# A grouped-query decode kernel: the values of the last three pairs multiplied in narrow pieces, and the last load cut in six

## The chip, the cores and the metric

The kernel runs on one core of one Trainium2 chip. The metric is the device time of one execution in microseconds (us), as a median over runs. Everything is float32.

## The reference

A decode step: eight sequences, one new token each. Attention with 32 query heads over 8 key/value heads and 8192 cached positions, plus a token-mixing block and the input itself. Cut to what matters:

```
x  = A_x                                        # 8 x 1 x 512
xn = layernorm(x)
q  = xn @ wq                                    # 32 heads of 128
s  = q . k_cache * 128**-0.5                    # per sequence and head, 8192 positions
p  = softmax(s)
o  = p . v_cache                                # per sequence and head, 128 wide
out = x + concat(o) @ wo + mixer(xn)            # mixer: layernorm, x*w1 + b1, gelu, times w2, sum, + b2
```

The key and the value cache hold 8 x 8 x 8192 x 128 numbers each, 512 MB together. They are read once.

## The kernel before

**Pairs and chunks.** The work is 64 pairs `i` of one key/value head and one sequence (`N_IT`). A pair has a key tile and a value tile of 4 MB each, [128 partitions x 64 tokens x 128], loaded by one DMA each into a ring of five buffers (`RING`, tile name `raw`). A pair is worked on in four chunks (`NCH`) of 16 tokens per partition (`CH_T`), so the whole has 256 chunks `n`. The DMAs are issued from SP, in an order sorted ahead; each waits until its ring buffer has been read for the last time. The very last load, the values of pair 63, goes out in five DMAs: 32 tokens of each partition, then 16, 8, 4 and 4.

**One step of the loop.** Step `s` transposes the keys of chunk `s+1` on TensorE (`t_half`, L202, copied out of PSUM by ACT and DVE at L203), multiplies the keys of chunk `s` with the query (`qk`, L220), and multiplies the values of chunk `s-9` with the softmax weights (`pv`, `LAG` = 9). Hooks hung on the steps do the softmax of a pair (`sm_max`, `sm_bias` L233, `sm_exp` L242, `sm_place` L249/L250, `sm_sum` L257), put a finished pair into its place (`o_place`, L301, L303), and project a finished head (`o_project`, L309). The order of instructions on each engine is that of this code. After step 255 no keys are left, and the steps hold only `pv` and hooks.

**The values product.** A float32 matmul stands as two records in the trace, and so does its weight load. In `pv` a chunk is four matmuls (`j`), each with 32 columns of weights (a slice of `PT`: four key tokens `u` times four heads, and 16 columns that nobody reads) and 512 wide moving values (four tokens of 128). They go to four column groups of the array, 32 columns each, which the rows show as the form 128*32, and run side by side. Of a result only the blocks count in which the weight's token and the value's token are the same. They stand in four places of a 512 wide PSUM tile: ACT copies and scales it at L289, and `o_place` picks the blocks with four matmuls against the selector `ohu` and adds them up. The last chunk alone (n = 255) is cut further: each of its four matmuls is done as four of 128 wide moving values (L281), which go to column group `u`, with the same weights and still a 512 wide result. Its copy out of PSUM is done in two halves of 256.

**The end.** Pair 63 is followed by `o_place(63)`, the projection of the last head (L309), an addition on DVE (L311) and the store of the output (L391).

Of the kernel before, what the change touches and what calls it, by code (L numbers as in the profile page):

```python
# [8 lines left out]
F32 = mybir.dt.float32  # L9
AF = mybir.ActivationFunctionType  # L10
# [4 lines left out]
B, D, HQ, HKV, SK, DH, F = 8, 512, 32, 8, 8192, 128, 1792  # L15
REP = HQ // HKV
P = 128
NT = SK // P
CH_T = 16
NCH = NT // CH_T  # L20
CG = 4
GT = CH_T // CG
GW = P // CG
# [5 lines left out]
N_IT = B * HKV  # L29
NK = N_IT * NCH  # L30
ZO = (NCH - 1) * 2 * REP
ZW = ZO + GW
PW = CG * NCH * GT * REP
LAG = 9
RING = 5

# [2 lines left out]
def attn_mixer_kernel(ctx: ExitStack, tc: tile.TileContext, x, kc, vc, wq, wo, w1, b1, w2, b2, out):  # L39
    nc = tc.nc  # L40
    const = ctx.enter_context(tc.tile_pool(name="const", bufs=1))
# [10 lines left out]
    def misc():  # L52
        return ps_m.tile([P, 512], F32, name="misc")
# [4 lines left out]
    for i in range(N_IT):  # L58
        order.append((i * NCH - 1, kc, KR, i))
        order.append((i * NCH + LAG, vc, VR, i))  # L60
    order.sort(key=lambda o: -o[0])

    def load_next():
        if order:
            _, src, to, i = order.pop()
            h, b = divmod(i, B)
            t = ring.tile([P, NT, DH], F32, name="raw")
            rows = src[b, h].rearrange("(p t) d -> p t d", p=P)
            first, last = to is KR and not i, not order
            at = 0  # L70
            for n in (CH_T,) * NCH if first else (NT // 2, CH_T, 2 * GT, GT, GT) if last else (NT,):
                nc.sync.dma_start(t[:, at:at + n, :], rows[:, at:at + n, :])
                if first and not at:
                    load_wq(0)
                at += n
            to[i] = t
# [3 lines left out]
    def load_wq(h):  # L80
        w = REP * DH
        t = one.tile([P, NC, w], F32, name="wqo")
        nc.sync.dma_start(t, wq[:, h * w:(h + 1) * w].rearrange("(c p) n -> p c n", p=P))
        wqs[h] = t

    def load_wo(h):
        t = one.tile([P, REP, D], F32, name="wqo")
        nc.sync.dma_start(t, wo[h * REP * DH:(h + 1) * REP * DH, :].rearrange("(r p) n -> p r n", p=P))
        wos[h] = t

    load_next()
    x_sb = t2k.tile([B, D], F32, name="t2k")
    nc.scalar.dma_start(x_sb, x.rearrange("b s d -> (b s) d"))
# [6 lines left out]
    for _ in range(RING - 1):  # L100
        load_next()
# [7 lines left out]
    ident = const.tile([P, P], F32, name="ident")  # L109
    make_identity(nc, ident)  # L110

    oh = const.tile([P, REP], F32, name="oh")
    nc.vector.tensor_reduce(oh, ident.rearrange("p (g h) -> p h g", h=REP), AX.X, ALU.add)
    ohw = t2k.tile([P, P], F32, name="t2k")
# [25 lines left out]
        Z.append(z)  # L140
    PT = []
    for k in range(2):
        t = const.tile([P, PW + GW - GT * REP], F32, name=f"pt{k}")
        nc.vector.memset(t, 0.0)
        PT.append(t)
    OTS = []
    for k in range(2):
        t = const.tile([P, REP, GW], F32, name=f"ot{k}")
# [45 lines left out]
    def t_half(n, k):  # L194
        if n >= NK:
            return
        if k == 0:
            KT[n] = ktp.tile([P, CH_T * P], F32, name="kt")
        w = CH_T // 2
        pt = ps_t.tile([P, w * P], F32, name="pt")  # L200
        for t in range(w):
            nc.tensor.transpose(pt[:, t * P:(t + 1) * P], KR[n // NCH][:, n % NCH * CH_T + k * w + t, :], ident)  # L202
        (nc.vector.tensor_copy if k else nc.scalar.copy)(KT[n][:, k * w * P:(k + 1) * w * P], pt)  # L203
        if k and n % NCH == NCH - 1:
            del KR[n // NCH]
            load_next()
# [38 lines left out]
    def sm_place(i):  # L245
        p = st[i][0]
        m = misc()
        for u in range(GT):
            nc.tensor.transpose(m[:, u * P:(u + 1) * P], p[:, u * P:(u + 1) * P], ident)  # L249
        nc.scalar.copy(PT[i % 2][:, :PW].rearrange("p (x u h) -> p x u h", u=GT, h=REP),  # L250
                       m.rearrange("p (u x k h) -> p x k u h", u=GT, k=2, h=REP)[:, :, 0])

    RL = {}
# [9 lines left out]
    O, OB = {}, {}  # L263

    def pv(n):
        if not 0 <= n < NK:
            return
        i, c = divmod(n, NCH)
        if c == 0:
            O[i] = ps_a.tile([P, 512], F32, name="acc")  # L270
        v = VR[i][:, c * CH_T:(c + 1) * CH_T, :].rearrange("p t d -> p (t d)")
        for j in range(CG):
            o = (j * NCH + c) * GT * REP
            w = PT[i % 2][:, o:o + GW]
            if n < NK - 1:
                nc.tensor.matmul(O[i][j * GW:(j + 1) * GW, :], w, v[:, j * 512:(j + 1) * 512],  # L276
                                 start=(c == 0), stop=(c == NCH - 1))
            else:
                for u in range(GT):
                    x = slice(u * DH, (u + 1) * DH)  # L280
                    nc.tensor.matmul(O[i][u * GW:(u + 1) * GW, x], w, v[:, j * 512 + u * DH:j * 512 + (u + 1) * DH],  # L281
                                     start=False, stop=(j == CG - 1))
        if c == NCH - 1:
            del VR[i]
            load_next()
            ob = t2k.tile([P, 512], F32, name="t2k")
            o, rl = O.pop(i), RL.pop(i)
            for x in ((slice(0, 512),) if n < NK - 1 else (slice(0, 256), slice(256, 512))):
                nc.scalar.activation(ob[:, x], o[:, x], AF.Copy, scale=rl)  # L289
            OB[i] = ob  # L290

    OT = {}
# [1 line left out]
    def o_place(i):  # L294
        h, b = divmod(i, B)
        if b == 0:
            OT[h] = OTS[h % 2]
        m = misc()
        ob = OB.pop(i)
        for u in range(GT):  # L300
            nc.tensor.matmul(m[:, :REP], ob[:, u * DH:(u + 1) * DH], ohu[:, u * REP:(u + 1) * REP],  # L301
                             start=(u == 0), stop=(u == GT - 1))
        nc.vector.tensor_copy(OT[h][:, :, BS * b], m[:, :REP])  # L303

    def o_project(h):
# [36 lines left out]
    def at(s, k, f, *a):  # L342
        hooks.setdefault((s, k), []).append((f, a))

    for i in range(N_IT):
        s = (i + 1) * NCH
        at(s - 1, 2, sm_max, i)
        at(s, 3, sm_bias, i)
        at(s + 1, 1, sm_exp, i)
        at(s + 1, 3, sm_place, i)  # L350
        at(s + 2, 3, sm_sum, i)
        at(s + LAG + (2 if i < N_IT - 2 else 0), 3, o_place, i)
    HS = B * NCH
    for h in range(HKV):
        s = h * HS
        if h + 1 < HKV:
            at(s + LAG + 4, 3, load_wq, h + 1)
            at(s + LAG + 9, 2, q_project, h + 1)
            at(s + LAG + 10, 2, q_place, h + 1)
        at(s + LAG + 12, 3, load_wo, h)  # L360
        at(s + HS + LAG + 3, 2, o_project, h)
# [18 lines left out]
    for s in range(NK + LAG + 4):  # L380
        for k in range(4):
            if k < 2:
                t_half(s + 1, k)
            elif k == 2:
                qk(s)
            else:
                pv(s - LAG)
            for f, a in hooks.pop((s, k), []):
                f(*a)
# [29 lines left out]
```

## Time and profile before

| | |
|---|---|
| median of 3 runs | 1308.89 us (1308.6 to 1309.88) |
| the profiled execution, its own time | 1308.48 us |
| its span, first to last instruction | 1306.7 us |
| mean granted TensorE clock | 0.957 |
| busy share PE / PE weight loads / DVE / ACT / POOL | 89% / 55% / 31% / 45% / 17% |
| read from HBM | 553.69 MB, 424 GB/s over the span |

PE is TensorE's matmul side, PEld its weight loads, DVE is VectorE, ACT ScalarE, POOL GpSimd, SP the engine that issues the large DMAs. The span is what the trace shows; the profiled execution's time is 1.8 us longer than it.

### The profile page before, as it was taken

What the parts mean: (1) busy time and instruction counts of PE and PEld (TensorE: products, weight loads), DVE (VectorE), ACT (ScalarE), POOL (GpSimd) and SP (SyncE); (2) the same over time, 40 slices, a digit from 0 to 9 for tenths busy, and PEclk for the clock granted to TensorE, in tenths of its full rate; (3) what the DMA queues carried; (4) which work ended last, traced back from release to release, by engine and by line L of the source; (5) the groups of instructions that cost most, each with busy time, mean ns of one, the idle gap of its engine ahead of it and who ended that gap; (6) DMA issues with size and microseconds to landing.
All of it is one profiled execution on the core that took longest, in us unless ns stands there. A gap on an engine that the chain in (4) does not pass through costs nothing.

```text
span 1306.7 us, 22347 instructions
## 1 busy us (share of the span) xinstructions
PE 1162.4 (89%) x9852; PEld 715.8 (55%) x9852; DVE 407.4 (31%) x646; ACT 587.8 (45%) x740; POOL 227.0 (17%) x242
## 2 busy tenths in 40 slices
PE   6979899798998989979898898998989979899988
PEld 4545555455554655546555555554645546555554
DVE  4423233232332333323333233322323323233321
ACT  2654244552545525445254452554525535255532
POOL 1322002220122201222012220122201221012310
PEclk8999999998999999999999898999989989899999
DMA  9999999999999999999999999999999999999995
GB/s 402 432 431 431 428 430 432 429 429 433 432 431 428 429 431 432 432 433 427 433 432 430 430 429 433 433 431 429 429 431 430 433 429 432 432 432 432 432 427 223
DMA packets 28164, 555.13 MB, mean 425 GB/s; under 512 B 2556, under 2 KB 2588, under 8 KB 11172
## 3 DMA queue, kind: packets, MB, share of 16 engines
q1 hardware_dynamic: 27924, 553.67, 98.8%
q8 instruction: 77, 1.26, 0.4%
q14 instruction: 19, 0.16, 0.0%
q0 software_dynamic: 128, 0.02, 0.0%
q10 hardware_dynamic: 16, 0.02, 0.0%
HBM read 553.69 MB, written 0.02 MB: 424 GB/s over the span
## 4 chain that ended last, share of the span: by engine, by line
DMA 56%; PE 39%; ACT 3%; DVE 1%; issue 1%; POOL 0%; SPq 0%; ACTq 0%; DVEq 0%; POOLq 0%
DMA raw<-in_A_k_cache_dram 37%; DMA wqo<-in_A_wq_dram 17%; PE pt L202 16%; PE acc L220 8%; PE acc L276 8%; PE misc L301 3%; DMA raw<-in_A_v_cache_dram 3%; PE misc L177 1%; ACT L242 1%; PE misc L249 1%; ACT kt L203 1%; ACT t2k L242 1%; PE misc L318 1%; PE misc L257 1%; PE misc L309 1%
## 5 line engine op out<-in xcount | busy, mean ns | idle before, releaser
L202 PE MATMUL pt<-ident,raw 128*128 128x128 f32 x4096 | 515.9, 281 | 67.6 <-DMA raw<-in_A_k_cache_dram 67.1
L202 PEld LDWEIGHTS pt<-ident,raw 128*128 128x128 f32 x4096 | 478.0, 147 | 74.5 <-issue 56.0
L203 DVE COPY kt<-pt 128x1024 f32<-128x1024 f32 x256 | 313.5, 1225 | 618.3 <-PE pt L202 505.4
L203 ACT COPY kt<-pt 128x1024 f32<-128x1024 f32 x256 | 258.8, 1011 | 455.7 <-PE pt L202 322.9
L220 PE MATMUL acc<-kt,z 128*32 128x512 f32 x2048 | 279.0, 617 | 0.0
L276 PE MATMUL acc<-raw,pt 128*32 128x512 f32 x2040 | 273.0, 608 | 2.5 <-DMA raw<-in_A_v_cache_dram 2.5
L329 POOL TENSOR_SCALAR g<-g,w2t 128x512 f32<-128x512 f32 x112 | 77.5, 692 | 876.6 <-ACT g L328 876.6
L276 PEld LDWEIGHTS acc<-raw,pt 128*32 128x32 f32 x2040 | 65.3, 113 | 143.6 <-issue 118.1
L330 POOL TENSOR_TENSOR macc<-macc,g 128x512 f32<-128x512 f32 x112 | 142.3, 1271 | 9.3
L328 ACT ACTIVATE g<-hb,b1t,w1t 128x512 f32<-128x512 f32 x112 | 91.1, 813 | 11.5 <-POOL macc L330 10.9
L289 ACT ACTIVATE t2k<-acc,rl 128x512 f32<-128x512 f32 (+1 forms) x65 | 44.0, 679 | 108.5 <-PE acc L276 104.6
L301 PEld LDWEIGHTS misc<-ohu,t2k 128*128 128x128 f32 x512 | 61.9, 191 | 55.0 <-DVE kt L203 31.0
L249 PEld LDWEIGHTS misc<-ident,t2k 128*128 128x128 f32 x256 | 26.8, 140 | 82.5 <-ACT t2k L242 76.7
L301 PE MATMUL misc<-ohu,t2k 128*128 128x4 f32 x512 | 67.3, 255 | 0.7 <-ACT t2k L289 0.6
L220 PEld LDWEIGHTS acc<-kt,z 128*32 128x32 f32 x2048 | 40.7, 109 | 44.5 <-issue 44.4
L249 PE MATMUL misc<-ident,t2k 128*128 128x128 f32 x256 | 42.0, 286 | 25.5 <-ACT t2k L242 25.5
L242 ACT ACT_TABLE_LOAD x48 | 61.6, 1283 | 0.8
L328 ACT ACT_TABLE_LOAD x48 | 61.6, 1283 | 0.8
L257 PEld LDWEIGHTS misc<-lr,ohl 128*128 128x128 f32 x128 | 20.1, 197 | 59.1 <-issue 50.7
L177 PE MATMUL misc<-wqo,xnT 128*32 128x128 f32 x256 | 15.5, 420 | 38.8 <-DMA wqo<-in_A_wq_dram 38.3
L250 ACT COPY pt<-misc 128x256 f32<-128x256 f32 x64 | 23.7, 370 | 58.1 <-PE misc L249 58.1
L233 PEld LDWEIGHTS misc<-ident,mr 128*128 128x128 f32 x128 | 19.0, 187 | 53.7 <-DVE kt L203 38.6
(67 smaller groups left out, 285.6 us busy)
## 6 DMA issues: line engine op xcount, KB each, us to landing
raw<-in_A_k_cache_dram SPq DMA_DIRECT2D x63, 4096.0 KB, 30.0
raw<-in_A_v_cache_dram SPq DMA_DIRECT2D x63, 4096.0 KB, 33.2
wqo<-in_A_wq_dram SPq DMA_DIRECT2D x8, 1024.0 KB, 30.6
wqo<-in_A_wo_dram SPq DMA_DIRECT2D x8, 1024.0 KB, 28.3
raw<-in_A_k_cache_dram SPq DMA_DIRECT2D x4, 1024.0 KB, 10.2
raw<-in_A_v_cache_dram SPq DMA_DIRECT2D x1, 2048.0 KB, 29.1
raw<-in_A_v_cache_dram SPq DMA_DIRECT2D x1, 1024.0 KB, 31.2
raw<-in_A_v_cache_dram SPq DMA_DIRECT2D x1, 512.0 KB, 31.9
```

The source lines that it names most:

```text
L202: nc.tensor.transpose(pt[:, t * P:(t + 1) * P], KR[n // NCH][:, n % NCH * CH_T + k * w + t, :], ident)
L203: (nc.vector.tensor_copy if k else nc.scalar.copy)(KT[n][:, k * w * P:(k + 1) * w * P], pt)
L220: nc.tensor.matmul(S[i][j * GW:(j + 1) * GW, :], w, kt[:, j * 512:(j + 1) * 512], start=(c == 0), stop=(c == NCH - 1))
L242: nc.scalar.activation(p, S.pop(i), AF.Exp, bias=st[i], scale=SCALE, accum_out=lr)
L249: nc.tensor.transpose(m[:, u * P:(u + 1) * P], p[:, u * P:(u + 1) * P], ident)
L257: nc.tensor.matmul(m[:, :1], ohl, st.pop(i)[1], start=True, stop=True)
L276: nc.tensor.matmul(O[i][j * GW:(j + 1) * GW, :], w, v[:, j * 512:(j + 1) * 512], start=(c == 0), stop=(c == NCH - 1))
L289: nc.scalar.activation(ob[:, x], o[:, x], AF.Copy, scale=rl)
L301: nc.tensor.matmul(m[:, :REP], ob[:, u * DH:(u + 1) * DH], ohu[:, u * REP:(u + 1) * REP], start=(u == 0), stop=(u == GT - 1))
L328: nc.scalar.activation(g, hb, AF.Gelu_apprx_tanh, bias=b1t[:, j:j + 1], scale=w1t[:, j:j + 1])
L329: nc.gpsimd.tensor_scalar(g, g, w2t[:, j:j + 1], 1.0, op0=ALU.mult, op1=ALU.mult)
L330: nc.gpsimd.tensor_add(acc, acc, g)
```

## The change

For the last three pairs (61, 62 and 63; `FINE` = 61) every chunk is done with 16 matmuls of 128 wide values in place of four of 512 (three chunks of pair 63, and all of 61 and 62, had four; the last chunk had 16). The weights slice now begins at the token's own four columns, so the wanted four rows of the result stand at the start of column group `u`, and all tokens of all chunks of a pair accumulate into the same [128 x 128] of PSUM. ACT copies 128 columns instead of 512 (for the last pair: one copy of 128 in place of two of 256), and `o_place` needs one matmul instead of four. `PT` is 12 columns wider, so that the last slice stays inside it; what lies behind it in SBUF moves (in the built program the ring's first buffer starts at byte 29,568 of a partition, 29,440 before). The last load's first DMA of 32 tokens becomes two of 16.

```diff
+FINE = N_IT - 3
...
-            for n in (CH_T,) * NCH if first else (NT // 2, CH_T, 2 * GT, GT, GT) if last else (NT,):
+            for n in (CH_T,) * NCH if first else (CH_T, CH_T, CH_T, 2 * GT, GT, GT) if last else (NT,):
...
-        t = const.tile([P, PW + GW - GT * REP], F32, name=f"pt{k}")
+        t = const.tile([P, PW + GW - REP], F32, name=f"pt{k}")
...
-            w = PT[i % 2][:, o:o + GW]
-            if n < NK - 1:
-                nc.tensor.matmul(O[i][j * GW:(j + 1) * GW, :], w, v[:, j * 512:(j + 1) * 512],
+            if i < FINE:
+                nc.tensor.matmul(O[i][j * GW:(j + 1) * GW, :], PT[i % 2][:, o:o + GW], v[:, j * 512:(j + 1) * 512],
                                  start=(c == 0), stop=(c == NCH - 1))
-            else:
-                for u in range(GT):
-                    x = slice(u * DH, (u + 1) * DH)
-                    nc.tensor.matmul(O[i][u * GW:(u + 1) * GW, x], w, v[:, j * 512 + u * DH:j * 512 + (u + 1) * DH],
-                                     start=False, stop=(j == CG - 1))
+                continue
+            for u in range(GT):
+                w = PT[i % 2][:, o + u * REP:o + u * REP + GW]
+                x = slice((j * GT + u) * DH, (j * GT + u + 1) * DH)
+                nc.tensor.matmul(O[i][u * GW:(u + 1) * GW, :DH], w, v[:, x],
+                                 start=(c == 0 and j == 0), stop=(c == NCH - 1 and j == CG - 1))
...
+            w = 512 if i < FINE else DH
             ob = t2k.tile([P, 512], F32, name="t2k")
-            o, rl = O.pop(i), RL.pop(i)
-            for x in ((slice(0, 512),) if n < NK - 1 else (slice(0, 256), slice(256, 512))):
-                nc.scalar.activation(ob[:, x], o[:, x], AF.Copy, scale=rl)
+            nc.scalar.activation(ob[:, :w], O.pop(i)[:, :w], AF.Copy, scale=RL.pop(i))
...
-        for u in range(GT):
+        n = GT if i < FINE else 1
+        for u in range(n):
             nc.tensor.matmul(m[:, :REP], ob[:, u * DH:(u + 1) * DH], ohu[:, u * REP:(u + 1) * REP],
-                             start=(u == 0), stop=(u == GT - 1))
+                             start=(u == 0), stop=(u == n - 1))
```

PE's order at its end, before, from `sm_sum(63)` on (`acc<-raw,pt` is `pv`, `misc<-ohu,t2k` is `o_place`, `misc<-wqo,ot` the last projection; pairs 61 and 63 use `pt_151`, pair 62 uses `pt_149`, and the shapes are those of the result):

```order
L257 MATMUL misc<-lr,ohl 128x1
L276 MATMUL acc<-raw,pt_149 32x512 x4
L301 MATMUL misc<-ohu,t2k 128x4 x4
L276 MATMUL acc<-raw,pt_149 32x512 x4
L276 MATMUL acc<-raw,pt_151 32x512 x4
L301 MATMUL misc<-ohu,t2k 128x4 x4
L276 MATMUL acc<-raw,pt_151 32x512 x8
L281 MATMUL acc<-raw,pt_151 32x128 x16
L301 MATMUL misc<-ohu,t2k 128x4 x4
L309 MATMUL misc<-wqo,ot_155 32x128 x16
```

and now, at the same place:

```order
L259 MATMUL misc<-lr,ohl 128x1
L283 MATMUL acc<-raw,pt_149 32x128 x16
L303 MATMUL misc<-ohu,t2k 128x4
L283 MATMUL acc<-raw,pt_149 32x128 x16
L283 MATMUL acc<-raw,pt_151 32x128 x16
L303 MATMUL misc<-ohu,t2k 128x4
L283 MATMUL acc<-raw,pt_151 32x128 x48
L303 MATMUL misc<-ohu,t2k 128x4
L311 MATMUL misc<-wqo,ot_155 32x128 x16
```

Nothing has changed its place; each `pv` is 16 narrow matmuls and each of the three `o_place` is one matmul. Lines 32 and later have moved by one or two.

ACT's last rows before (the three copies of pairs 61, 62 and 63 are `t2k<-acc,rl`; `t2k,lr<-acc,nb` is `sm_exp(63)`):

```order
L289 ACTIVATE t2k<-acc,rl 128x512
L242 ACTIVATE t2k,lr<-acc,nb 128x512
L250 COPY pt_151<-misc 128x256
L289 ACTIVATE t2k<-acc,rl 128x512
L289 ACTIVATE t2k<-acc,rl 128x256 x2
```

and now:

```order
L290 ACTIVATE t2k<-acc,rl 128x128
L244 ACTIVATE t2k,lr<-acc,nb 128x512
L252 COPY pt_151<-misc 128x256
L290 ACTIVATE t2k<-acc,rl 128x128 x2
```

The copies are narrower, and the last two have become one. On SP the one row `raw<-in_A_v_cache_dram 128x4096` ahead of the last `128x2048` has become two of `128x2048`; DVE and POOL have the rows that they had.

## Rows read from the trace of the kernel before

**Rows 1.** The page: GB/s in 40 equal slices; a DMA queue: packets, MB, share.

```profile
GB/s 402 432 431 431 428 430 432 429 429 433 432 431 428 429 431 432 432 433 427 433 432 430 430 429 433 433 431 429 429 431 430 433 429 432 432 432 432 432 427 223
...
q8 instruction: 77, 1.26, 0.4%
```

**Rows 2.** Stretches: busy time by engine, granted clock, DMA share, GB/s.

```profile
1270.00:1284.00 14.00, 13.50 (x126) 8.31 (x122) 5.22 (x9) 4.77 (x7) 0.00 (x0) 1.00 0.99 424
1284.00:1298.50 14.50, 14.28 (x118) 6.09 (x114) 2.11 (x9) 2.50 (x5) 0.00 (x0) 1.00 0.51 212
```

**Rows 3.** The chain that ended last, its end: start us, us, what.

```profile
1242.59 36.84 DMA raw<-in_A_v_cache_dram
1279.43 0.14 issue
...
1292.24 0.31 PE misc L257 x2
...
1293.55 0.99 PE misc L301 x8
...
1296.40 1.06 PE misc L301 x8
...
1299.31 0.92 PE acc L281 x32
```

**Rows 4.** SP: DMA of pair 62's values, first and last of pair 63's.

```profile
1257.94 0.33 SPq L72 DMA_DIRECT2D raw<-in_A_v_cache_dram  x1
...
1264.85 0.33 SPq L72 DMA_DIRECT2D raw<-in_A_v_cache_dram  x1
...
1267.36 0.43 SPq L72 DMA_DIRECT2D raw<-in_A_v_cache_dram  x1
```

**Rows 5.** The same three DMAs: KB each, us to landing.

```profile
raw<-in_A_v_cache_dram SPq DMA_DIRECT2D x1, 4096.0 KB, 31.2
...
raw<-in_A_v_cache_dram SPq DMA_DIRECT2D x1, 2048.0 KB, 29.1
...
raw<-in_A_v_cache_dram SPq DMA_DIRECT2D x1, 256.0 KB, 31.7
```

**Rows 6.** L281: ns minimum, median, maximum; first and last start.

```profile
L281 PE MATMUL acc<-raw,pt x32: 272/272/273, 1299.1 to 1299.9; 128*32 128x128 f32 x32
```

**Rows 7.** Timeline: PE in the last pairs, and what follows it.

```profile
1289.31 1.06 PE L276 MATMUL acc<-raw,pt 128*32 128x512 f32 x8
...
1294.46 1.92 PE L276 MATMUL acc<-raw,pt 128*32 128x512 f32 x16
...
1297.38 1.92 PE L276 MATMUL acc<-raw,pt 128*32 128x512 f32 x16
1299.12 1.06 PE L281 MATMUL acc<-raw,pt 128*32 128x128 f32 x32
...
1300.25 0.84 ACT L289 ACTIVATE t2k<-acc,rl 128x256 f32<-128x256 f32 x2 [3.90 <-PE acc L281]
...
1300.77 1.05 PE L301 MATMUL misc<-ohu,t2k 128*128 128x4 f32 x8 [0.59 <-ACT t2k L289]
1301.87 0.17 DVE L303 COPY ot<-misc 128x4 f32<-128x4 f32 x1 [4.21 <-PE misc L301]
```

**Rows 8.** A copy of 128 columns out of PSUM on ACT (L180).

```profile
L180 ACT COPY sq<-misc x8: 265/265/265, 17.6 to 1070.3; 128x128 f32<-128x128 f32 x8
```

**Rows 9.** Timeline: one matmul (L257) and DVE, which waits for it.

```profile
1292.17 0.38 PE L257 MATMUL misc<-lr,ohl 128*128 128x1 f32 x2
...
1292.59 0.17 DVE L259 RECIPROCAL rl<-misc 128x1 f32<-128x1 f32 x1 [2.87 <-PE misc L257]
```

**Rows 10.** L177, 32 matmul records of the narrow form; that stretch.

```profile
1068.34 1.93 PE L177 MATMUL misc<-wqo,xnT 128*32 128x128 f32 x32 [5.51 <-DMA wqo<-in_A_wq_dram]
...
1068.30:1070.30 2.00, 1.96 (x36) 1.93 (x40) 0.00 (x0) 0.00 (x0) 0.00 (x0) 0.50 1.18 508
```

## The prediction

> **What bounds the kernel now.** I read the page first, for what is full all the time. The bytes moved per slice stand at 427 to 433 GB/s from the second slice to the last but one, and fall to 223 in the last [rows 1]: the caches stream at a constant rate, and engines that work less in the middle win nothing. The change does nothing there. It lies in the last 27 us, so the question is what sets the end. The stretches answer the first half: up to 1284 us the DMA engines are busy 0.99 of the time, from 1284 to 1298.5 only 0.51 at 212 GB/s, while PE is busy 14.28 of 14.5 us at a granted clock of 1.00, the 2.4 GHz level [rows 2]. The stream is ragged: about half of the DMA engines are through, and the other half carry the last tile in.
>
> The chain of waits gives the second half. It follows a value DMA to 1279.43, goes 0.14 us later to PE, and stays with PE (short steps of ACT between) to the end of the last chunk at 1299.31 + 0.92 = 1300.23 [rows 3]. By that alone PE sets the end, and each microsecond taken from it would count in full. So I looked at the transfers that the chain doesn't name. Pair 62's values were issued at 1257.94, the first and the last piece of pair 63's at 1264.85 and 1267.36 [rows 4]; 31.2, 29.1 and 31.7 us later they had landed [rows 5], at 1289.14, 1293.95 and about 1299.0. The last chunk's matmuls began at 1299.12 [rows 6, 7]. So PE and the last 256 KB arrive there together, and a faster PE finds a wall 0.1 us ahead of it. That is what the reader is to see: the chain names one bound, and a second stands right behind it.
>
> **The change, part by part.**
>
> *The narrow matmuls.* Eleven chunks go from 8 records of 512 to 32 of 128; the last chunk has the form already, so it has a price in this trace. Its 32 records of 272 ns start from 1299.12 to 1299.9 [rows 6], 0.027 us apart, 0.86 us for the chunk. The two wide chunks ahead of it started at 1297.38 [rows 7], so a wide one takes 1.74 / 2 = 0.87. Start to start the two forms cost the same; counted to the end of the chunk, as the chain does, it is 0.92 [rows 3], 0.05 more. I take 0.03, between the two, so 11 x 0.03 = 0.33 us more for PE, with 0 and 0.55 as bounds. The weights slices differ now from matmul to matmul, but the last chunk loads them for each matmul anyway.
>
> A rule stands against this part. TensorE: Matmul & The Clock Gate, Back-to-back issue gap, in the Trainium skill, gives for a stream of weight load and matmul about 81 ns a matmul at a width of 128 and 131 at 512. By it a narrow chunk would take 32 x 81 = 2.6 us, and the sum would come out near 17 us on the other side. The row above shows 27 ns a record where four column groups take turns, so the sum goes by the row.
>
> *o_place of pairs 61 and 62.* Four matmuls become one. The four cost 0.99 and 1.06 us of PE on the chain; a single matmul between the same neighbours (L257, two records) costs 0.31 [rows 3]. PE gains 0.68 + 0.7 = 1.38.
>
> *What of it is on the path.* The first four narrow chunks, of pair 61, come before anything is gained, so pair 62's first chunk, at 1289.31 now [rows 7], is 0.12 late: its data are there since 1289.14. The softmax of pair 63 hangs on this, and moves by about as much. Then the two o_place fall in, and PE would be at the last chunk 1.38 - 0.33 = 1.05 us earlier, at 1298.07, and at its last quarter (8 records, token group j = 3) 0.64 later, at 1298.7. The data of that quarter land at 1299.0. With the 0.14 us from landing to PE [rows 3] and 0.07 for an extra piece (below) it starts at 1299.2, and PE has waited half a microsecond. Seven starts of 0.027 and 0.27 for the last record bring its end to 1299.66. It was 1300.23: **0.57 us gained**, of the 1.05 that PE had to give.
>
> *The tail.* From PE's end at 1300.23 DVE's copy followed at 1301.87 [rows 7]: two halves of the copy on ACT from 1300.25 on, and the four matmuls from 1300.77. Now ACT copies 128 columns. The nearest row is a copy of that shape out of PSUM at 0.265 us [rows 8]. One matmul and its release of DVE take 1292.59 - 1292.17 = 0.42 [rows 9]. With the hand-overs of 0.02 and 0.04 that the timeline shows now this is 0.02 + 0.27 + 0.04 + 0.42 = 0.75 us in place of 1.64: **0.89 us gained**. Projection, addition and store are untouched.
>
> *Six pieces.* The first DMA, 2 MB, becomes two of 1 MB. SP issues it in 0.33 us [rows 4], some 30 us ahead of its landing, so one issue more costs nothing; without that cover it would be 0.33. What it can give: pair 63's first chunk could start when half of the 2 MB is in. But it runs second of the two chunks that start at 1294.46 [rows 7], so at 1295.3 now and at about 1294.8 then, and the whole 2 MB is there at 1293.95. Worth nothing while PE is 0.8 us later than that. What it can cost: shorter rows. The 4.2 MB of 62 and the 2.1 MB behind it landed 4.81 us apart, and I have no row for the same bytes in halves; from nothing to 0.2, I take 0.07, which the wait above holds already.
>
> *The wider weights tile* costs 12 columns in a memset 1250 us before the end.
>
> **Sum.** 0.57 + 0.89 = 1.46 us. The profiled execution took 1308.48 us, its span 1306.7: 1305.24 for the span, 1307.02 for the execution. That execution was 0.4 under the median of the three runs and just under the fastest. I put the forecast at 1307.2, between 1307.0 and 1307.4, the median less the same sum.
>
> **The rivals.** What a measurement of this kernel can tell from no change is about 0.2%, 2.6 us, so the forecast itself lies inside that.
>
> *PE's gain counts in full.* If the landing is a little earlier in an execution, or narrow chunks cost nothing, the last chunk ends 1.05 to 1.38 earlier: 1.9 to 2.3 us in sum, 1306.2 to 1306.6. Against it stands the landing at 1299.0, which nothing here brings forward.
>
> *The last landing comes later.* PE's program grows by 11 x 48 - 3 x 12 = 492 records. The page shows a queue that brings instructions, 77 packets with 1.26 MB [rows 1]: 64 bytes for each of the 19,704 records of matmuls and weight loads, so two packets more, each 0.4% x 16 x 1306.7 / 77 = 1.1 us of one DMA engine. If they fall on an engine that carries the last piece, ahead of it, the end moves by up to 1.1 us, and 0.4 us are left of the gain: 1308.1.
>
> *The narrow matmuls don't keep the pace,* and the kernel is slower. One chunk in a row is not twelve. There is a row for 32 records of this form that took 1.93 us [rows 10], with the clock at 0.50, the 1.2 GHz level, after a wait of 5.5 us. If chunks cost, say, 1.51 (PE's weight loads kept it that busy there), it is 0.65 more in each of 12 chunks, 7.8 less 1.38 and 0.89: 5.5 us slower, 1314. The gain is gone at 0.17 more per chunk (half a microsecond of wait to fill, then the 1.46, over 11); past 0.41 the loss can be measured. For it speaks that a denser stretch of instructions is not in the trace; against it the 0.86 us of the last chunk, and a clock of 1.00 through the end, with no wait of PE over 0.5 us to come.
>
> *The stream slows down.* All ring buffers start 128 bytes further, off a multiple of 256. DMA: Bandwidth & Descriptors, How a descriptor splits into AXI transactions, in the Trainium skill, says that a descriptor that starts off such a boundary pays for the bytes below its start; no row of this trace shows whether that holds for a destination. As a mechanism of this kernel: one part in 128 more on each 32 KB row, on a stream of some 1290 us, is 10 us, 1317.
>
> **Chances.** Forecast, gain between 1.0 and 1.8: 0.66. PE in full: 0.10. Later landing: 0.12. Narrow matmuls slow: 0.05, half of it past what can be measured. Stream slower: 0.03. The stream faster by an accident of its own, over 2.6 us in all: 0.04. Faster by over 0.2%: 0.06, the last case and a part of the second; slower: 0.06; the rest, 0.88, within. The range from 1305.9 to 1309.0 takes in the first three cases and the scatter of 0.6 us about a median.
>
> **What would show it.** In the changed kernel's trace: 32 records a chunk at 0.86 to 0.92 us, chunk after chunk; o_place at 0.3 us; PE waiting up to half a microsecond for a value DMA shortly before 1299.2, where it waited for none; the last piece landing within 0.2 us of 1299.0; ACT's last copy at 0.27 and DVE's copy 0.75 after PE's end. The forecast is wrong if the last landing moves by more than 0.5 us, if PE stalls between narrow chunks without a semaphore, or if GB/s in the middle slices leaves 427 to 433.

## The result, and the profile after

The changed kernel takes **1314.40 us** (median of six runs, 1313.96 to 1315.08) where the kernel before, timed beside it, takes 1308.86 (1308.60 to 1309.88). The ratio is 1.0043, with an interval from 1.0033 to 1.0053: slower by 5.5 us, about 0.4%. The forecast was 1307.2, with a range up to 1309.0. It was wrong, and on the side that its rival on the stream had.

I read the page first. Of after, the GB/s in 40 slices, and the queue that brings instructions, as in [rows 1]:

```profile
GB/s 400 430 427 429 427 430 430 426 427 430 430 428 426 427 431 430 430 427 426 431 429 430 427 423 434 430 427 429 423 434 430 430 430 423 431 430 430 430 426 230
...
q8 instruction: 79, 1.29, 0.4%
```

Slice by slice this is hard to tell from [rows 1]; a 430 stands where a 432 stood. Slices of 423, 426 and 434 leave the 427 to 433 that the prediction had set as a sign of being wrong, but a single slice is a poor sign: the changed kernel with its ring back in place (the second experiment), whose stream is as fast as before, has slices of 426 and 437. One long stretch says it better. The stretch from 100 to 1250 us (busy time by engine, granted clock, DMA share, GB/s), of before:

```profile
100.00:1250.00 1150.00, 1033.28 (x8721) 636.24 (x8714) 355.63 (x542) 522.79 (x657) 201.90 (x209) 0.96 1.00 431
```

and of after:

```profile
100.00:1250.00 1150.00, 1031.47 (x8709) 636.38 (x8701) 355.30 (x541) 522.09 (x656) 200.03 (x207) 0.96 1.00 429
```

The DMA engines are busy all the time in both, and move 429 instead of 431 GB/s. This is a stretch in which the diff changes no loop: by the code, nothing happens in it that didn't happen before. Two parts in 431 of a stream of about 1290 us are 6.0 us, roughly, since both figures are rounded. The engines' busy times have hardly moved, and the granted clock is 0.96 in both.

The chain that ended last (start us, us, what), after, from the landing of pair 61's values to the end:

```profile
1248.66 37.31 DMA raw<-in_A_v_cache_dram
1285.96 0.14 issue
...
1300.17 0.32 PE misc L303 x2
1300.49 1.88 PE acc L283 x64
1302.37 0.32 PE misc L303 x2
1302.69 1.21 PE acc L283 x35
1303.90 0.81 issue
1304.70 1.97 PE acc L283 x61
1306.67 0.02 issue
1306.70 0.38 ACT t2k L290
1307.07 0.04 issue
1307.12 0.40 PE misc L303 x2
1307.52 0.02 issue
1307.54 0.18 DVE ot L305
```

Three things are to be seen against [rows 3] and [rows 7]. Pair 61's values land at 1248.66 + 37.31 = 1285.97 instead of 1279.43: the whole loss, 6.5 us, is there before the first narrow matmul runs. The end of the chain is shorter, as forecast: one `o_place` takes 0.32 us (0.99 and 1.06 in [rows 3]), two narrow chunks take 1.88. And between the 35th and the 36th of the last 96 records PE stops for 0.81 us and waits for nothing that the profile shows. No line of before answers to that. The prediction had named such a stall, and a last landing more than 0.5 us later, as signs that it is wrong; both are here.

The last bytes follow the stream. Stretches of half a microsecond (the last figure is GB/s), of before:

```profile
1298.50:1299.00 0.50, 0.50 (x8) 0.13 (x4) 0.00 (x0) 0.00 (x0) 0.00 (x0) 1.00 0.01 4
1299.00:1299.50 0.50, 0.50 (x20) 0.38 (x16) 0.00 (x0) 0.00 (x0) 0.00 (x0) 1.00 0.00 0
```

and of after:

```profile
1305.00:1305.50 0.50, 0.50 (x29) 0.50 (x22) 0.00 (x0) 0.00 (x0) 0.00 (x0) 1.00 0.01 4
1305.50:1306.00 0.50, 0.50 (x28) 0.50 (x22) 0.00 (x0) 0.00 (x0) 0.00 (x0) 1.00 0.17 33
```

The last bytes of the values move between 1298.5 and 1299.0 before, and between 1305.0 and 1305.5 after. The 33 GB/s behind them in the changed kernel are no values. The DMA queues from 1305.5 to 1306.0 (packets, MB, share) have one line:

```profile
q8 instruction: 1, 0.02, 17.4%
```

It is a single packet of instructions, and it comes 1.1 us after the end of PE's stop. From pair 61's landing to the end of the span it was 1306.7 - 1279.43 = 27.27 us, and is 1312.4 - 1285.97 = 26.43: 0.84 us gained behind the landing, 6.54 lost ahead of it, 5.7 in sum, as the spans say.

### The profile page after: what moved, and what is told of

It is laid out like the page before. It is cut to its first block, busy times and chain, and to the rows that moved or that the text cites. A ratio compares the mean times of both kernels' runs of the same rounds, so it can differ in the third digit from the quotient of the medians.

```text
span 1312.4 us, 22838 instructions
## 1 busy us (share of the span) xinstructions
PE 1162.8 (89%) x10098; PEld 724.9 (55%) x10098; DVE 407.2 (31%) x646; ACT 586.8 (45%) x739; POOL 227.1 (17%) x242
## 3 DMA queue, kind: packets, MB, share of 16 engines
q1 hardware_dynamic: 28068, 553.67, 98.8%
## 5 line engine op out<-in xcount | busy, mean ns | idle before, releaser
L277 PE MATMUL acc<-raw,pt 128*32 128x512 f32 x1952 | 260.7, 606 | 2.7 <-DMA raw<-in_A_v_cache_dram 2.6
L290 ACT ACTIVATE t2k<-acc,rl 128x512 f32<-128x512 f32 (+1 forms) x64 | 42.9, 670 | 108.7 <-PE acc L277 94.7
```

The lines of the kernel that those rows point to most:

```text
L277: nc.tensor.matmul(O[i][j * GW:(j + 1) * GW, :], PT[i % 2][:, o:o + GW], v[:, j * 512:(j + 1) * 512], start=(c == 0), stop=(c == NCH - 1))
L290: nc.scalar.activation(ob[:, :w], O.pop(i)[:, :w], AF.Copy, scale=RL.pop(i))
```

## Experiments: where the loss sits

**My theory** after this: the ring's first byte stands at 29,568 of a partition instead of 29,440, which is 115 x 256; the loads now write to addresses off a multiple of 256 bytes, and each row that a DMA writes pays for it. **Rivals:** something in the narrow code (its 492 records, its instruction fetches) slows the stream; another tile that moved, not the ring, does it; any shift does it, or any odd size, not just one off 256.

**Only the wider tile**, in the kernel before; all of the pairs' code as it was:

```
-        t = const.tile([P, PW + GW - GT * REP], F32, name=f"pt{k}")
+        t = const.tile([P, PW + GW - REP], F32, name=f"pt{k}")
```

> The kernel before with one edit: the two weights tiles are 12 columns wider, as in the changed kernel, and nothing else. The ring's first buffer starts at byte 29,568, 128 off a multiple of 256. Address theory (the load stream is slower because every ring buffer has moved by 128 bytes): about 1315, 5.5 to 6.8 us slower than before, last value piece landing near 1305.5 instead of 1299.0, GB/s in the middle slices 423 to 431 instead of 427 to 433. Rival (the 5.5 us come from the narrow matmuls, by their longer PE program or their pace): no change, 1308.9 within 0.7 us.

Measured: 1314.95 (1314.71 to 1315.61) against 1308.88; ratio 1.0046, 1.0033 to 1.0060. Twelve columns that are never read cost 6.1 us, with not one instruction more on PE's queue. The narrow code is out as the cause of the loss.

**The change with the ring at home.** In the changed kernel `spread`, a tile of 128 bytes in a partition, goes to a pool behind the ring. The ring begins at 29,440 again:

```
-    spread = const.tile([B, GW], F32, name="spread")
+    spread = one.tile([B, GW], F32, name="spread")
```

> The changed kernel, with the ring back at its old place: a 128-byte constant of the prologue (spread) is moved from the pool ahead of the ring to one behind it, so the ring's first buffer starts at 29,440 again, and the tiles of wq/wo too. Address theory: the stream is that of before, last landing 1299.0 to 1299.2, and the change shows its own worth: 0.8 to 1.5 us faster than before (1307.4 to 1308.1), the smaller figure if PE stalls for 0.8 us near its end as it does in the changed kernel (0.81 us that no semaphore explains). Rival (narrow matmuls): as slow as the changed kernel, about 1314.4.

Measured: **1307.46** (1307.18 to 1308.30) against 1308.88; ratio 0.9990, 0.9981 to 0.9999. The stretch from 100 to 1250 us in this kernel:

```profile
100.00:1250.00 1150.00, 1026.98 (x8725) 633.58 (x8718) 355.48 (x542) 523.62 (x657) 202.43 (x209) 0.96 1.00 431
```

The stream is back at 431 GB/s, and all of the change is in. Together with the run ahead of it this settles that the step of memory makes the loss: the tile without the code has it, the code without the shift doesn't.

**Half the shift.** The kernel before, its second `PT` 16 columns wider: the ring at 29,504, 64 bytes off a multiple of 256.

```
-        t = const.tile([P, PW + GW - GT * REP], F32, name=f"pt{k}")
+        t = const.tile([P, PW + GW - GT * REP + 16 * k], F32, name=f"pt{k}")
```

> The kernel before, with the second weights tile 16 columns wider, so that the ring starts 64 bytes further, at 29,504. Address theory: slower than before; by the full 5.5 to 6.8 us if all that counts is whether the start is a multiple of 256, by something else if the distance counts (a multiple of 128 already lost is then worse or no better: 3 to 8 us). Rival: no change, 1308.9.

Measured: 1315.16 (1314.90 to 1315.48) against 1308.88; 1.0047, 1.0034 to 1.0061. The same 6.3 us as with 128 bytes; the loss doesn't grow with the distance.

**The other way.** The kernel before with `spread` behind the ring (the same line as above), so that the ring begins 128 bytes earlier, at 29,312.

> The kernel before, with the same 128-byte constant moved behind the ring: everything from the ring on starts 128 bytes earlier, the ring at 29,312, again 128 off a multiple of 256. Address theory by distance to a multiple of 256: 5.5 to 6.8 us slower than before, like the 128 bytes further. If instead the place as such or a fuller SBUF mattered: no change, 1308.9. Rival (narrow matmuls): 1308.9.

Measured: 1315.45 (1314.94 to 1316.04) against 1308.88; 1.0049, 1.0033 to 1.0064. Not a wider tile, and not a later start: 128 bytes off in either direction cost the same.

**A whole 256.** The kernel before with `spread` and the two 64-byte tiles `w1t` and `b1t` behind the ring, which begins at 29,184 (114 x 256).

```
-    w1t = const.tile([P, NF], F32, name="w1t")
-    b1t = const.tile([P, NF], F32, name="b1t")
+    w1t = one.tile([P, NF], F32, name="w1t")
+    b1t = one.tile([P, NF], F32, name="b1t")
-    spread = const.tile([B, GW], F32, name="spread")
+    spread = one.tile([B, GW], F32, name="spread")
```

> The kernel before with three constants (256 bytes in sum) moved behind the ring, so the ring starts at 29,184, 256 bytes earlier. Address theory by multiples of 256: no change, 1308.9 within 0.7 us, GB/s in the middle as before. Rival (it is the old place, 29,440, that is special, or multiples of 512 or more decide in some way; 29,184 is a multiple of 512 and 29,440 is not): some other time, such as 1315.

Measured: 1308.92 (1308.62 to 1309.69) against 1308.69; 1.0003, 0.9994 to 1.0012. No change. A shift as such costs nothing.

**The ring or its neighbours.** In all runs so far the tiles behind the ring moved with it. Two runs part them, with a new pool between ring and neighbours. In the first it holds `spread`: the ring alone moves, to 29,312.

```
+    gap = ctx.enter_context(tc.tile_pool(name="gap", bufs=1))
-    spread = const.tile([B, GW], F32, name="spread")
+    spread = gap.tile([B, GW], F32, name="spread")
```

> The kernel before; the 128-byte constant is moved into a pool of its own between the ring and the transposed keys. The five ring buffers start 128 bytes earlier (29,312), and all that stands behind them (transposed keys, the tiles of wq and wo, work tiles) keeps its place. If it is where the load DMAs write that counts: about 1315, 6 to 6.8 us slower than before. If it is where the engines read and write their own tiles, or where wq and wo land: 1308.9.

Measured: 1314.96 (1314.67 to 1315.20) against 1308.75; 1.0044, 1.0029 to 1.0060. Its long stretch:

```profile
100.00:1250.00 1150.00, 1025.81 (x8691) 631.74 (x8684) 354.05 (x540) 520.06 (x655) 199.92 (x207) 0.96 1.00 429
```

In the second the pool holds a spare tile of 128 bytes: the ring stays at 29,440, and everything behind it moves by 128.

```
+    spare = gap.tile([P, GW], F32, name="spare")
+    nc.vector.memset(spare, 0.0)
```

> The kernel before with a 128-byte tile more, between the ring and the transposed keys. The ring stays at 29,440, and all behind it starts 128 bytes further, as in the changed kernel (wq and wo at 210,368). If it is where the load DMAs write that counts: 1308.9 within 0.7 us; the wq and wo tiles are 3% of the bytes, 0.2 us by their share. If the place of the other tiles counts: about 1315.

Measured: 1308.76 (1308.43 to 1309.58) against 1308.75; 0.9998, 0.9989 to 1.0007. So it is the ring, the only tile of these that the cache loads write to. PE reads the ring too, from the same moved addresses; the two runs below speak to that.

**A price per row or per byte?** A load writes 128 rows of 32 KB, spread over 16 DMA engines; 128 loads make 1024 rows for each engine. 6.1 us over 1024 rows is 6 ns a row. With the loads cut into four (the first key tile and the last value tile were in pieces before), each engine writes 4096 rows of 8 KB and the same bytes: 24 us if the price hangs on the row, 6 if it hangs on the bytes.

```
-            ... else (NT // 2, CH_T, 2 * GT, GT, GT) if last else (NT,):
+            ... else (NT // 2, CH_T, 2 * GT, GT, GT) if last else (NT // 4,) * 4:
```

> The kernel before with every 4 MB load issued as four DMAs of 1 MB, rows of 8 KB in place of 32 KB, the ring at 29,440. It is the base for the next run. A cost per row shows as a slower stream: by pair 63's pieces in the run before, up to some 2%, 1310 to 1335, whatever the ring's place costs.

> The same with quartered loads, and the ring 128 bytes earlier (29,312). If the off-boundary ring costs a fixed time at each row's start or end, four times as many rows cost four times as much: 24 us over the run with quartered loads at the old place. If it costs by the byte: 6 us, as with whole loads.

Measured, against 1308.84: quarters with the ring at 29,440 take 1326.69 (1326.20 to 1326.86; 1.0135, 1.0115 to 1.0155); the same with `spread` behind the ring, at 29,312, take 1345.67 (1345.24 to 1345.77; 1.0280, 1.0260 to 1.0300). The difference is 18.98 us. The long stretch, of quarters at 29,440:

```profile
100.00:1250.00 1150.00, 1012.22 (x8681) 623.43 (x8673) 353.44 (x540) 519.28 (x652) 200.48 (x207) 0.95 1.01 425
```

and of quarters at 29,312:

```profile
100.00:1250.00 1150.00, 1007.24 (x8597) 622.38 (x8590) 348.85 (x532) 512.79 (x644) 195.34 (x202) 0.94 1.01 419
```

The gap is 6 GB/s where it was 2. It is a price per row in the main: 18.98 us over 4096 rows is 4.6 ns, against 6.0 with whole loads. PE reads the ring alike in both runs with quarters, and the loss is three times that of whole loads, so the reads are not what pays.

The traces' DMA records have a duration for each packet, and a row is one packet. Those of 32 KB take 1215.9 ns on average before and 1219.8 with the ring alone moved, 3.9 ns more; those of 8 KB take 310.0 with quarters at 29,440 and 314.5 at 29,312, 4.5 more. The rest of the 6 ns lies in other rows: the packets of 2 KB, nearly all of them of wq and wo, go from 85.0 to 87.6 ns with the ring alone moved, though their own tiles stayed in place. With 1008 large and 528 small packets an engine, 1008 x 3.9 + 528 x 2.6 ns are 5.3 of the 6.2 us. Why the small ones are slower beside a moved ring is open.

## Experiments: what the change itself gives

These runs all have `spread` behind the ring, so that the ring is at home, and are read against the first of them (1307.46). Its timeline (start us, us, engine, line, what, xcount) of PE in the last pairs:

```profile
1294.17 1.95 PE L283 MATMUL acc<-raw,pt 128*32 128x128 f32 x64
1296.05 0.39 PE L303 MATMUL misc<-ohu,t2k 128*128 128x4 f32 x2
1296.37 1.28 PE L283 MATMUL acc<-raw,pt 128*32 128x128 f32 x35
1298.01 1.94 PE L283 MATMUL acc<-raw,pt 128*32 128x128 f32 x61 [0.36 <-issue]
```

and of the weight loads (PEld) in the same place:

```profile
1296.37 1.02 PEld L283 LDWEIGHTS acc<-raw,pt 128*32 128x32 f32 x36
1298.01 1.09 PEld L283 LDWEIGHTS acc<-raw,pt 128*32 128x32 f32 x40 [0.63 <-issue]
```

The landing of pair 61's values on its chain, and the chain's end:

```profile
1242.73 36.98 DMA raw<-in_A_v_cache_dram
1279.71 0.14 issue
...
1296.44 1.21 PE acc L283 x35
1297.65 0.36 issue
1298.01 1.97 PE acc L283 x61
1299.98 0.02 issue
...
1300.84 0.17 DVE ot L305
```

PE begins the last three chunks at 1296.37, where it was 1297.38 [rows 7]: 1.01 us earlier. Then both kinds of record stop at once, behind the 35th matmul record, with no semaphore named: the matmuls are idle for 0.36 us, the weight loads for 0.63. It is the stop of 0.81 us of the changed kernel, at the same record. It costs more than the idle time of the matmuls. The last 96 records take 1299.98 - 1296.44 = 3.54 us here and 1306.67 - 1302.69 = 3.98 in the changed kernel, and 2.80 where none stops (the next run): 0.74 and 1.18 us.

Behind this stop, too, one packet of instructions follows. The stretch, and the DMA queues in it:

```profile
1299.00:1299.50 0.50, 0.50 (x28) 0.50 (x22) 0.00 (x0) 0.00 (x0) 0.00 (x0) 1.00 0.13 33
...
q8 instruction: 1, 0.02, 12.6%
```

**A tail alone: the last pair only.**

```
-FINE = N_IT - 3
+FINE = N_IT - 1
```

> The changed kernel with the ring at its old place (29,440), but only pair 63 narrow (FINE = 63); o_place of pairs 61 and 62 keeps its four matmuls. It takes away PE's gain ahead of the last chunk and leaves the tail's. By the prediction's terms: the last chunk ends near 1300.2 as before, the copy and the one matmul behind it still save 0.8 us, so about 1308.1, between the kernel before (1308.9) and the one with three narrow pairs (1307.5). Rival (the end follows the last landing alone): the same as with three pairs, 1307.5. No wait of PE inside its matmuls that a semaphore doesn't explain.

Measured: 1307.98 (1307.76 to 1308.35) against 1308.69; 0.9994, 0.9985 to 1.0003. 0.7 us less, by pair 63's copy and its one `o_place` if it is more than scatter: the interval takes in no change. Its chain has no stop:

```profile
1297.52 2.80 PE acc L283 x96
1300.32 0.02 issue
1300.35 0.38 ACT t2k L290
```

96 records in 2.80 us are 0.93 a chunk, sustained over three chunks.

**Two pairs.** `FINE = N_IT - 2`.

> The changed kernel with the ring at its old place and two narrow pairs (FINE = 62). PE keeps 0.68 us of its gain less than with three (o_place of pair 61 has four matmuls again), but its program is 180 records shorter, and the block boundary at record 20,161 falls into the last projection, behind 256 records that take longer than in the run with three pairs. By the last landing (1299.0) and the block theory: no stop, the last chunk ends near 1299.8 to 1300.0, 1307.2 to 1307.6, the same as with three pairs. If PE's own work still set the end: 1307.9, close to the run with one narrow pair.

Measured: 1308.02 (1307.76 to 1308.76) against 1308.75; 0.9994, 0.9985 to 1.0003. A miss: I had expected it near three pairs. Its chain shows no stop in the 96 records either, and they end at 1300.04:

```profile
1297.24 2.80 PE acc L283 x96
1300.04 0.02 issue
```

Its span is 1305.8 us, as short as that of three pairs (1305.7); but its profiled execution took 1308.55, 2.7 us more than the span, where it is 1307.48 - 1305.7 = 1.8 with three pairs. All its eleven runs are like that, with 1.9 to 2.8 us outside the span, where the runs of every other kernel here have 1.7 to 1.9. No instruction lies out there, but the DMA records go on, and they have one packet, 1.7 us behind the span's end. The stretch, and the queues from 1306.5 to 1308:

```profile
1307.50:1308.00 0.50, 0.00 (x0) 0.00 (x0) 0.00 (x0) 0.00 (x0) 0.00 (x0) 0.50 0.16 33
...
q8 instruction: 1, 0.02, 5.3%
```

In no other profiled run does the instruction queue move anything behind the span. So the span is about as short as expected, and a late fetch of instructions may be what the time pays for; that the execution waits for this packet is not shown.

**The stop's place.** Twelve tiny matmuls at the start of the program, 48 records of PE with their loads, some 1300 us ahead of the stop. If the stop hangs on how many instructions came before, it moves 24 matmuls earlier; if it hangs on the data or the buffers, it stays.

```
+    m = misc()
+    for _ in range(12):
+        nc.tensor.matmul(m[:GW, :1], ident[:, :GW], ident[:, :1], start=True, stop=True)
```

> The changed kernel with the ring at its old place, and 12 tiny matmuls (48 records of PE) more at its start, while PE waits for the first keys. In the run without them PE stops for 0.36 us after the 35th narrow matmul behind the last but one o_place, with no semaphore to wait for. Theory that instructions arrive in blocks of 256 records and PE runs ahead of them: the stop moves 24 matmuls (48 records) earlier, to about the 11th, at a similar length of 0.2 to 1 us; the total stays at 1307.5 within 0.5. Rival (the stop belongs to that chunk, its data or its PSUM tile): it stays behind the 35th.

Measured: 1307.26 (1307.10 to 1307.92) against 1308.69; 0.9990, 0.9981 to 0.9999. Weight loads in the last three chunks:

```profile
1297.01 0.36 PEld L283 LDWEIGHTS acc<-raw,pt 128*32 128x32 f32 x12
1297.59 1.46 PEld L283 LDWEIGHTS acc<-raw,pt 128*32 128x32 f32 x55 [0.21 <-issue]
```

The stop stands behind the 12th load instead of the 36th, 24 earlier. It is shorter: the weight loads are idle for 0.21 us instead of 0.63, and the last three chunks take 3.13 us on the chain, 0.33 more than without a stop:

```profile
1297.08 3.13 PE acc L283 x96
```

So its place hangs on the count of instructions. That it is the fetch of the next block of them is my reading; no record names what PE waits for. What speaks for it is that a packet of the instruction queue starts 1.1 to 1.2 us after the end of each such stop: at 1305.82 in the changed kernel, 1299.15 with the ring at home, 1298.76 here, 1299.01 in the next run. The median is 0.2 us under that of the first run, too little to tell.

**Five pieces instead of six** of the last load:

```
-            ... else (CH_T, CH_T, CH_T, 2 * GT, GT, GT) if last else (NT,):
+            ... else (NT // 2, CH_T, 2 * GT, GT, GT) if last else (NT,):
```

> The changed kernel with the ring at its old place, and the last load in five pieces again (the first of 2 MB). By the prediction the sixth piece is worth nothing, since PE comes to pair 63's first chunk about 0.8 us after the whole 2 MB has landed: 1307.5, equal to the six-piece run within 0.2 us, the last landing up to 0.1 earlier. Rival (the split carries part of the gain): 0.3 to 0.8 us slower than it, with PE waiting for a value DMA ahead of pair 63's first chunk.

Measured: 1307.48 (1307.21 to 1308.21) against 1308.69; 0.9991, 0.9982 to 1.0000. The sixth piece is worth nothing, as forecast. The stop stays behind the 35th record:

```profile
1296.24 1.21 PE acc L283 x35
1297.45 0.49 issue
1297.94 1.97 PE acc L283 x61
```

## Why the prediction was wrong, step by step

**The step that failed** is "*The wider weights tile* costs 12 columns in a memset 1250 us before the end". It priced the tile's filling and not its size. The tile pushes the ring 128 bytes on, the loads' destination leaves a multiple of 256, and the stream, which the prediction had named as the bound of all but the last 27 us, slows by 6.1 us, as the tile alone shows (1314.95). Every other term of the sum lies in the last 27 us; this one is spread over 1290, which is why no row near the change hinted at it.

**The rival** *The stream slows down* described it, and had 0.03. Its place and its point (off a multiple of 256) were right. Its price was not: 10 us. Measured, it is 6.1 us, and by the packets 3.9 ns of 1216 for a row of 32 KB, one part in 310 where one in 128 was taken. The prediction's argument for so small a chance was that no row showed whether the rule holds for a destination. That is an unknown cost on the path that sets the end, with nothing that hides it, and it should have had more than a sentence: the range ended 8 us short of it. DMA: Bandwidth & Descriptors, How a descriptor splits into AXI transactions, in the Trainium skill, speaks of the first transaction of a read; the runs agree in direction for a destination in SBUF, with 64 and 128 bytes off alike.

**A rival that fits by chance.** *The narrow matmuls don't keep the pace* came to 1314, the measured time to the microsecond. It is not the cause: the wider tile without a narrow matmul takes 1314.95, and the narrow matmuls with the ring at home take 1307.46.

**The sum for the rest** came out: 1.46 us forecast, 1308.88 - 1307.46 = 1.42 measured with the ring at home, with an interval from 0.1 to 2.5. That it fits so closely is luck in part. Its terms fared less well, and by the two profiled spans it is 1.0:

- *Narrow matmuls*, 0.33 more for eleven chunks. Two chunks take 1.95 us on the timeline, the wide ones 1.92 [rows 7]: 0.015 a chunk, half of what was taken. Of the 81 ns that TensorE: Matmul & The Clock Gate, Back-to-back issue gap, in the Trainium skill, gives for a matmul of this width there is no sign: 2.80 us for 96 records are 29 ns.
- *o_place*, 0.31 each: 0.32. PE came 1.01 us earlier to the last three chunks; 1.05 were forecast at the last chunk.
- *The last chunk's end*, 0.57 earlier because it waits for the landing. The end is 1299.98 instead of 1300.23, 0.25 earlier. The stream of that execution was 0.28 behind, though (pair 61's values land at 1279.71 instead of 1279.43), and counted from that landing it is 0.53. The size is near, but not for the reason given: PE waited for no value DMA. The stop behind the 35th record took 0.74 of what PE had won. The stretch of the kernel with the ring at home in which the last bytes of the values move:

```profile
1298.50:1299.00 0.50, 0.50 (x28) 0.50 (x21) 0.00 (x0) 0.00 (x0) 0.00 (x0) 1.00 0.11 41
```

  PE is busy throughout, and its last quarter comes behind that. Without the stop the 96 records would have ended at 1296.44 + 2.80 = 1299.24, and their last quarter would have begun some half a microsecond before, about when the last bytes came in; the forecast wait would then have been likely, but no run shows it.
- *The tail*, 0.89. From PE's end to DVE's copy it is 0.86 us (1299.98 to 1300.84 on the chain with the ring at home; 0.87 on after's) instead of 0.75; 1.64 before: 0.78 gained. The copy on ACT takes 0.37, not the 0.27 of [rows 8]. Line L290 of after, ns minimum, median, maximum:

```profile
L290 ACT ACTIVATE t2k<-acc,rl x3: 367/367/367, 1295.7 to 1306.7; 128x128 f32<-128x128 f32 x3
```

  [rows 8] is a plain copy; this one multiplies by a column of scales, at the same shape. Half of the wide form's two copies [rows 7], 0.84 us for two of 256, or 0.42, would have been nearer.
- *Instruction fetches*: two packets more, 79, as forecast. I priced them as time on a DMA engine, ahead of the last landing. What they cost, if the stop is theirs, they cost on PE: 0.74 us with the ring at home, 1.18 in the changed kernel. The prediction named the sign ("if PE stalls between narrow chunks without a semaphore") and gave it no price.
- *Six pieces*, nothing: nothing.

0.25 + 0.78 = 1.03 us is what the two profiled spans differ by (1306.7 and 1305.7). The execution profiled of before was 0.4 under its median, which makes up the difference to 1.42. Counted from pair 61's landing, the span is 27.27 us before and 1305.7 - 1279.71 = 25.99 with the ring at home, 1.28 less.

**The version to take** is the change with `spread` behind the ring: 1307.46, 1.4 us faster than before (0.1 to 2.5 by the interval), 6.9 faster than the change as made.

## What to carry to other kernels

When a kernel is bound by a stream of loads, a change to the size of any tile ahead of the load buffers can change where the loads land: work out the first byte of the load buffers before and after, and keep it on a multiple of 256, by ordering the pools if need be. A price that no row shows, on the path that bounds the whole run, belongs in the range even when its chance looks small. A time that agrees with a rival's is no proof of that rival; a run that holds its cause alone is. Before bytes at the end of a trace are read as a load's, look at the queue that moved them. Take a duration from an instruction of the same operation, not just of the same shape.

## What the runs showed of the hardware

- A DMA from HBM whose destination in a partition starts 64 or 128 bytes off a multiple of 256 takes longer: a packet of 32 KB 1219.8 ns instead of 1215.9 (128 off; 1219.9 at 64), one of 8 KB 314.5 instead of 310.0 (128 off). Over this stream it is 6.1 to 6.6 us, and 18.98 with rows of 8 KB. 29,184 and 29,440 are alike, so 256 is enough.
- Cutting rows of 32 KB into 8 KB costs 1326.69 - 1308.84 = 17.85 us here, with every start on a multiple of 256. Four packets of 310.0 ns take 1240.0 instead of 1215.9, 8 ns for each further row of an engine; over 3072 further rows that would be 24.7 us, but the loads' queue also keeps the DMA engines busy for 99.5% of the span instead of 98.8%, which gives some of it back.
- Among the last 96 short matmul records (29 ns apart) PE stops once in four of the six kernels that have them, with no semaphore named: its weight loads are idle for 0.21 to 1.07 us, and the 96 records take 0.33 to 1.18 us more. The place moves with the number of instructions ahead of it, and a packet of the instruction queue follows 1.1 to 1.2 us behind the stop's end.
